# Two hundred DMA issues move from SyncE's queue to ScalarE's, and the attention tiles of the single blocks move to other steps

## The chip, the core and the metric

The kernel runs on one core of a Trainium2 chip. The metric is the device time of one execution in microseconds. Before the change the median of three runs is 741.4 us (740.5 to 743.21). The profile is of one further execution, which took 743.39 us; its instructions span 741.4 us.

## The reference

The kernel computes a chunked attention and, on its result, a mixer with two matrix products per axis:

```
S chunks of 64:  attn = softmax(q k^T / 8);  x = attn v          # 8 batches, 8 heads, 576 x 64
h = relu(x^T w_tok1) w_tok2;   u = x + h^T                       # token axis, 576 -> 256 -> 576
out = u + relu(u w_ch1) w_ch2                                    # channel axis, 512 -> 1536 -> 512
```

All data are float32. x has 512 channels (8 heads of 64), and the rows of a batch are its 576 tokens.

## The kernel before

**Tiles.** An attention tile is 128 rows by 512 columns, that is two chunks for all heads. There are 36 tiles, nine for each pair of batches. One tile takes: a load of q and k (512 KB) and of v (256 KB); the scores on TensorE (`ps_s`, or `ps_sv` L372); maximum, difference and sum on VectorE (L345, L348, L358); the exponential on ScalarE (L352); a transpose that is done by VectorE in 32 x 32 blocks (L395) and by a trip through DRAM, `far<-blocks` out (L400) and four transfers `pf<-far` back (L406); a ScalarE copy into `pt` (L423); the product with v (`ps_v` L442, or `ps_sv` L384); and a scaling into `x` (L463). The tile's x goes through the same kind of trip into `xt`, which the mixer reads.

**Stages.** Float32 products are made from a high and a low part (gh and gl, bh and bl). The profile has four stretches. In the first, to about 149 us, batch 0 is done and the weights are split; batch 1's four tiles are threaded through it by `STARTS`, whose rows are tiles and whose five columns are the steps of: scores and softmax; the trip to DRAM; the copy into `pt`; the product with v and the scaling; the end of the tile. Steps of this stretch count two for each of 12 features f (the first for `us[0]`, the second for `us[1]`), then one per f. In the second stretch, 149 to 335 us, two single blocks of 512 rows go through the channel products: 48 steps (`now`), an even one for `ch1` (12 matmuls, `ps_c` L682) and an odd one for `ch2` of the feature before (12 matmuls, `acc` L726). `BURSTS` lists the steps after which one attention step (a "burst") is issued: scores of tile `order[k]` and the product with v of tile `order[k-2]`, in one go. One step ahead of a burst stands `before` (the copy into `pt`), one step behind it `behind` (the four `pf<-far`). `TOKENS_AT` are the steps of the token products of batches 2, 3 and 4 (`ps_t` L581), `MIX_AT` those of the mix that opens the first pair (`ps_t` L653, VectorE u L660, and its splits L1091 to L1098). `SUMS` are the steps at which GpSimd adds halves of the channel weights into `sparts` (one buffer; L1008, L1017), ScalarE and GpSimd split them (L1023, L1024), and four transfers `w<-sparts` (`dump`, L881, two per step) take them to DRAM. The third and fourth stretch, to the end, are three pairs of blocks: each group of seven products (`ps_p` L1051) stands between halves of the second channel product (`acc` L1121), and each product needs its weights from the ring of eight buffers (`ring<-w`, `load_product`, L1041), which it asks for seven products ahead. `snap` (ScalarE L1140) takes a product out of one of two PSUM buffers.

**Order.** TensorE's order is the program's from step 35 of the first stretch on; in the steps before that a planner sets it. SyncE's (SP's) queue keeps the program's order throughout: one issue that waits holds all behind it. The orders of ScalarE, VectorE and GpSimd, after batch 0, are the planner's too; it works with its own estimates of costs; `issue_after(ins)` only says that something stands behind `ins` on its engine. All DMAs are issued from SP's queue. ScalarE's queue is in order as well.

Of the kernel before, what the change touches and what calls it, by code (L numbers as in the profile page):

```python
# [8 lines left out]
F32 = mybir.dt.float32  # L9
# [37 lines left out]
KH = 2 * P  # L47
RING = 8
LAG = 2
BURSTS = (2, 6, 9, 13, 17, 20, 23, 26, 30, 34, 37, 38, 40, 43)  # L50
PAIR_BURSTS = {0: (1, 9, 13, 19, 22, 30, 33, 38, 41), 1: (4, 11, 22, 28), 2: ()}
PAIR_GAPS = (1, 3)
SINGLE_GAPS = (1, 1)
TOKENS_AT = (19, 35, 44)
MIX_AT = (44, 45)
PAIR_TOKENS = ((4, 7), (4, 0), ())
PAIR_MIX = ((7, 9), (7, 9))
# [3 lines left out]
DUMPS = 2  # L61
# [16 lines left out]
END_FILL = (3, 2, 2, 3, 6, 1, 1)  # L78
STEP_FILL = (2, 4, 4, 4, 4, 4, 4, 2, 0, 2, 5, 3, 0, 8, 5, 4, 4, 5, 7, 4, 1, 1, 5, 3)

STARTS = ((9, 10, 10, 10, 14), (13, 14, 15, 16, 16), (17, 18, 18, 19, 22), (23, 23, 24, 26, 27))
SPLIT_AT = (30, 25, 32, 33, 30)
FIRST_TOKENS = (9, 10)
HAND_FROM = 11
# [2 lines left out]
JOBS = [(9, "ready")]  # L87
JOBS += [(s, "part", j, k) for j, ss in enumerate(STARTS) for k, s in enumerate(ss)]
JOBS += [(s, "split", i) for i, s in enumerate(SPLIT_AT)]
# [18 lines left out]
def attention_mixer_kernel(ctx, tc, qk_in, vo_in, v_in, w1_in, w2_in, wc1_in, wc2_in, out):  # L108
# [19 lines left out]
    nc = tc.nc  # L128
# [170 lines left out]
            xts[k] = pool.tile([P, N // BK, NDT, BK], F32, tag="xt", name="xt")  # L299
        return xts[k]  # L300

    def load_qk(i):
        qk = pool.tile([P, 2, NHP, P], F32, tag="qk" if i > 4 else "qk0", name="qk", bufs=3 if i > 4 else 5)
        nc.sync.dma_start(out=qk.rearrange("p a b c -> p (a b c)"), in_=qk_in[i])
        tiles[i] = {"qk": qk}

    def load_v(i):
        if i < NTILE:
            v = pool.tile([P, VPAD], F32, tag="v1" if i > 4 else "v0", name="v", bufs=2 if i > 4 else 5)
            v = v[:, :VW].rearrange("p (a b c) -> p a b c", a=2, c=DV)  # L310
            src = vo_in[i]
        else:
            v = pool.tile([P, 2, NHP, D], F32, tag="v", name="v", bufs=4)
            src = v_in[i - NTILE]
        nc.sync.dma_start(out=v.rearrange("p a b c -> p (a b c)"), in_=src)
        tiles[i]["v"] = v

    def attn_load(i):
        load_qk(i)
        load_v(i)  # L320

    def attn_s(i, src=None, tag="at"):
        t = tiles[i]
# [17 lines left out]
    def attn_p(i, fill=0):  # L341
        t = tiles[i]
        sv = t["s"]
        mx = per_row("mx")
        nc.vector.tensor_reduce(out=mx, in_=sv, axis=AX.X, op=ALU.max)  # L345
        convert(fill)
        pr = t["pr"] = pool.tile([P, DM], F32, tag="pr", name="pr")
        nc.vector.tensor_tensor(  # L348
            out=pr.rearrange("p (h a k) -> p a h k", a=2, k=CH), in0=sv,
            in1=mx.broadcast_to([P, 2, NHP, CH]), op=ALU.subtract,  # L350
        )
        nc.scalar.activation(out=pr, in_=pr, func=AF.Exp, scale=1.0 / float(D) ** 0.5)  # L352

    def attn_z(i):

        t = tiles[i]
        zi = t["zi"] = per_row("zs")
        nc.vector.tensor_reduce(  # L358
            out=zi, in_=t["pr"].rearrange("p (h a k) -> p a h k", a=2, k=CH), axis=AX.X, op=ALU.add
        )  # L360
        nc.scalar.activation(out=zi, in_=zi, func=AF.Copy, bias=1e-9)
        nc.vector.reciprocal(out=zi, in_=zi)

    def attn_both(i, j):

        ps = ps_at.tile([P, 2, 512], F32, tag="at", name="ps_sv")
        if i is not None:
            qk = tiles[i]["qk"]
            for hp in range(NHP):
                for a in range(2):  # L370
                    for c in range(2):
                        nc.tensor.matmul(  # L372
                            ps[c * CH:(c + 1) * CH, a, hp * CH:(hp + 1) * CH],
                            lhsT=qk[a * D:(a + 1) * D, 0, hp, c * CH:(c + 1) * CH],
                            rhs=qk[a * D:(a + 1) * D, 1, hp, c * CH:(c + 1) * CH],
                            start=True, stop=True,
                        )
            tiles[i]["s"] = ps[:, :, :NHP * CH].rearrange("p a (h k) -> p a h k", k=CH)
        if j is not None:
            t = tiles[j]  # L380
            for hp in range(NHP):
                for a in range(2):
                    for c in range(2):
                        nc.tensor.matmul(  # L384
                            ps[c * CH:(c + 1) * CH, a, (NHP + hp) * D:(NHP + hp + 1) * D],
                            lhsT=t["pt"][a * CH:(a + 1) * CH, hp, c * CH:(c + 1) * CH],
                            rhs=t["v"][a * CH:(a + 1) * CH, c, hp, :D],
                            start=True, stop=True,
                        )
            t["pv"] = ps[:, :, NHP * D:2 * NHP * D].rearrange("p a (h d) -> p a h d", d=D)  # L390
# [155 lines left out]
    def load_waiting(n):  # L546

        while waiting and n > 0:
            n -= load_x(*waiting.pop(0))
# [8 lines left out]
    def batch_tiles(b):  # L558
        base = (b // 2) * NTILE
        return [base + j for j in (range(0, 5) if b % 2 == 0 else range(5, 9))]  # L560
# [198 lines left out]

    first = batch_tiles(0)  # L760
    load_qk(first[0])
    fetch(1)
    load_v(first[0])
# [48 lines left out]
    for engine in engines:  # L812
        ins = [i for i in nc.cur_bb.bb.instructions if i.engine == engine][-1]
# [4 lines left out]
    order = [t for b in range(2, B) for t in sorted(batch_tiles(b), key=lambda t: t % NTILE != 4)]  # L818
# [55 lines left out]
    wide = ctx.enter_context(tc.tile_pool(name="wide", bufs=1, space=bass.MemoryType.DRAM))  # L874
    stored, tokens, dumps = {}, {}, []

    def dump(n):

        for key, src in dumps[:n]:
            stored[key] = wide.tile([P, 2, KH], F32, tag="w{}_{}".format(*key), name="w")  # L880
            nc.sync.dma_start(out=stored[key], in_=src if src.dtype == F32 else src.bitcast(F32))  # L881
        del dumps[:n]

# [47 lines left out]
    def attention(k):  # L931

        i = order[k] if k < len(order) else None
        j = order[k - LAG] if k >= LAG else None
        attn_both(i, j)
        if k + 2 < len(order):
            attn_load(order[k + 2])
        load_waiting(1)
        if i is not None:
            attn_p(i)  # L940
            tiles[i]["far"] = far_out(tiles[i]["pr"])
            attn_z(i)
        ready = len(waiting)
        if j is not None:
            attn_o(j)
            attn_end(j)
        load_waiting(min(2, ready))
# [88 lines left out]
    products = [(p, n) for _ in range(PAIRS) for p in range(NFC // 2) for n in range(7)]  # L1036

    def load_product(upto):
        for i in range(len(ring), min(upto, len(products))):
            w = pool.tile([P, 2, KH], F32, tag="ring", name="ring", bufs=RING)  # L1040
            nc.sync.dma_start(out=w, in_=stored[products[i]])  # L1041
            ring.append(w)

    def product(i, u, width):
# [205 lines left out]

    single_events = plan_bursts(BURSTS, len(FIRST_QK), *SINGLE_GAPS)
    events, taken = {}, len(FIRST_QK) + len(BURSTS)
    for n in range(PAIRS):
        events[n] = plan_bursts(PAIR_BURSTS[n], taken, *PAIR_GAPS)
        taken += len(PAIR_BURSTS[n])
    for k in range(SINGLE):
        at, width = BLOCKS[k]
        accs, pend = [], None
        for f in range(NFC):
            for half in range(2):  # L1260
                if half == 0:
                    g = ch1(u, f, width=width)
                elif pend is not None:
                    ch2(*pend)
                if half == 1:
                    pend = (S + at, width, u, f, g, accs)
                now = 2 * (NFC * k + f) + half
                if now in TOKENS_AT:
                    b = 2 + TOKENS_AT.index(now)
                    batch_split(b)  # L1270
                    if b != 3:
                        load_waiting(99)
                    rs[b] = [tok1(b, m) for m in range(NT1)]
                if now in MIX_AT:
                    mix_pair(SINGLE, rs, MIX_AT.index(now))
                if now == OPEN_AT[0]:
                    open_x(1)
                if now == OPEN_AT[1]:
                    open_x(SINGLE, SINGLE + 1)
                if RING_AT <= now < RING_AT + RING - 1:  # L1280
                    load_product(now - RING_AT + 1)
                if now in TOKENS_TO:
                    store_token()
                for kind, at_k in single_events.get(now, ()):
                    calls[kind](at_k)
                dump(DUMPS)
                for p, (add, cut, put) in enumerate(SUMS):
                    for when, step in ((add, add_sums), (cut, split_sums)):
                        if now == when:
                            with in_turn():  # L1290
                                step(p)
                    if now == put:
                        dump_sums(p)
        dump(len(dumps) if k else 1)
        if k == 0:
            u = turn(1, rs)
        ch2(*pend)
# [57 lines left out]
```

## Time and profile before

| | |
|---|---|
| median of three runs | 741.4 us (740.5 to 743.21) |
| the profiled execution | 743.39 us |
| its span | 741.4 us |
| TensorE busy (PE) | 717.3 us, 97% |
| VectorE, ScalarE, GpSimd busy | 437.1, 275.4, 189.6 us |
| DMA | 139.94 MB, mean 189 GB/s |
| chain that ended last | PE 74%, DMA 8%, DVE 6%, ACT 5%, SPq 4% |

PE is a matmul, DVE is VectorE, ACT is ScalarE, POOL is GpSimd, SP is SyncE; a name with q is the engine's queue (an issue or a wait), which isn't counted as busy. The granted clock (PEclk) is the share of TensorE's full speed. "Idle before" is an engine's time without work ahead of an instruction, and the arrow names what ended it.

### The profile page before, as it was taken

How to read it: one execution, taken by the hardware profiler on the slowest of the kernel's cores; microseconds unless marked ns; L12 is line 12 of the kernel's file. 1: busy time of each engine (PE TensorE's matmuls, PEld its weight loads, DVE VectorE, ACT ScalarE, POOL GpSimd, SP SyncE). 2: the span in 40 equal slices, each digit the busy share in tenths (PEclk: the TensorE clock that was granted, in tenths of full speed). 3: DMA queues.
4: the chain of work that ended last, by engine and by line, in shares of the span. 5: the costliest groups of instructions: out<-in, count | busy, mean ns of one | idle time of the engine just before them, and what ended most of it. 6: DMA issues, size and time to landing. Idle time of an engine off the chain costs nothing.

```text
span 741.4 us, 14629 instructions
## 1 busy us (share of the span) xinstructions
PE 717.3 (97%) x5730; PEld 629.7 (85%) x5730; DVE 437.1 (59%) x735; ACT 275.4 (37%) x505; POOL 189.6 (26%) x161
## 2 busy tenths in 40 slices
PE   6899998999999999989999999999999999999997
PEld 4488898988889877878888888988888899999997
DVE  4799966555546546577666763686343539433361
ACT  5899953333332333332333333332211324112120
POOL 0000012162346543103111163061112602311220
PEclk8999999999999999999999999999999999999999
DMA  9956346669855676745888995045655430644111
GB/s 344 407 218 222 118 157 198 218 202 290 289 178 185 202 229 224 237 127 197 268 261 272 284 312 139 12 140 161 192 177 182 138 93 21 235 135 126 53 54 53
DMA packets 93268, 139.94 MB, mean 189 GB/s; under 512 B 10832, under 2 KB 44880, under 8 KB 93200
## 3 DMA queue, kind: packets, MB, share of 16 engines
q1 hardware_dynamic: 93200, 139.02, 57.0%
q8 instruction: 45, 0.74, 0.4%
q14 instruction: 23, 0.19, 0.1%
HBM read 98.34 MB, written 39.71 MB: 186 GB/s over the span
## 4 chain that ended last, share of the span: by engine, by line
PE 74%; DMA 8%; DVE 6%; ACT 5%; SPq 4%; issue 2%; POOL 0%; DVEq 0%; ACTq 0%; POOLq 0%
PE acc L1121 24%; PE ps_p L1051 21%; PE acc L726 8%; PE ps_c L682 7%; PE ps_t L653 5%; PE ps_t L581 4%; SPq L406 2%; DMA far<-blocks 2%; PE ps_sv L372 2%; PE ps_sv L384 1%; DMA raw_t<-in_w 1%; DVE wtop L225 1%; ACT low L206 1%; PE sum L590 1%; ACT wtop L205 1%
## 5 line engine op out<-in xcount | busy, mean ns | idle before, releaser
L1121 PE MATMUL acc<-gh,kept_c 128*128 128x512 f32 (+1 forms) x576 | 169.5, 376 | 0.0
L1051 PE MATMUL ps_p<-bh,ring 128*128 128x512 f32 (+1 forms) x504 | 148.5, 376 | 0.1
L1121 PEld LDWEIGHTS acc<-gh,kept_c 128*128 128x128 f32 x576 | 108.2, 189 | 12.8
L1121 PE MATMUL acc<-gl,kept_c 128*128 128x512 f32 (+1 forms) x288 | 107.9, 375 | 0.0
L1051 PEld LDWEIGHTS ps_p<-bh,ring 128*128 128x128 f32 x504 | 94.6, 189 | 11.8 <-DVE sum L1146 0.5
L1051 PE MATMUL ps_p<-bl,ring 128*128 128x512 f32 (+1 forms) x252 | 94.4, 375 | 0.0
L726 PE MATMUL acc<-gh,kept_c 128*128 128x288 f32 (+1 forms) x384 | 91.1, 341 | 1.7 <-ACT gh L695 1.5
L484 POOL TENSOR_TENSOR xl<-x,xh 128x512 fp32r<-128x512 f32 x28 | 37.7, 1358 | 160.4 <-ACT xh L483 137.2
L726 PEld LDWEIGHTS acc<-gh,kept_c 128*128 128x128 f32 x384 | 63.7, 192 | 8.2 <-ACT gh L695 2.8
L1148 POOL TENSOR_TENSOR sum<-snap,sum 128x512 f32<-128x512 f32 (+1 forms) x18 | 23.1, 1282 | 167.4 <-ACT snap L1140 144.7
L1121 PEld LDWEIGHTS acc<-gl,kept_c 128*128 128x128 f32 x288 | 54.4, 189 | 6.5
L682 PE MATMUL ps_c<-uh,kept_c 128*128 128x512 f32 x192 | 57.8, 383 | 1.3 <-DVE rl L600 1.3
L726 PE MATMUL acc<-gl,kept_c 128*128 128x288 f32 (+1 forms) x192 | 57.1, 336 | 0.0
L1051 PEld LDWEIGHTS ps_p<-bl,ring 128*128 128x128 f32 x252 | 47.6, 189 | 5.7
L1153 ACT ACTIVATE gh<-c 128x512 fp32r<-128x512 f32 (+1 forms) x36 | 22.4, 622 | 77.3 <-DVE c L1146 73.4
L352 ACT ACTIVATE pr<-pr 128x512 f32<-128x512 f32 x36 | 22.6, 628 | 76.6 <-DVE pr L348 76.6
L1140 ACT COPY snap<-ps_p 128x512 f32<-128x512 f32 (+1 forms) x36 | 20.8, 577 | 75.5 <-PE ps_p L1051 71.9
L1154 DVE SCALAR_TENSOR_TENSOR gl<-g,gh 128x512 fp32r<-128x512 f32 (+1 forms) x36 | 32.9, 936 | 24.4 <-ACT gh L1153 24.4
L696 DVE SCALAR_TENSOR_TENSOR gl<-ps_c,gh 128x512 fp32r<-128x512 f32 (+1 forms) x36 | 21.8, 605 | 40.1 <-ACT gh L695 40.0
L682 PE MATMUL ps_c<-both,kept_c 128*128 128x288 f32 x288 | 41.2, 291 | 1.0 <-DVE gl L696 1.0
L682 PEld LDWEIGHTS ps_c<-uh,kept_c 128*128 128x128 f32 x192 | 35.7, 189 | 6.8 <-DVE rl L600 1.7
L682 PEld LDWEIGHTS ps_c<-both,kept_c 128*128 128x128 f32 x288 | 37.2, 189 | 2.2 <-DVE gl L696 1.4
(134 smaller groups left out, 1257.8 us busy)
## 6 DMA issues: line engine op xcount, KB each, us to landing
ring<-w SPq DMA_DIRECT2D x126, 256.0 KB, 4.0
qk<-in_qk SPq DMA_DIRECT2D x36, 512.0 KB, 4.8
far<-blocks SPq DMA_DIRECT2D x63, 256.0 KB, 2.9
raw_c<-in_wc SPq DMA_DIRECT2D x24, 512.0 KB, 9.3
pf<-far SPq DMA_DIRECT2D x124, 64.0 KB, 2.4
v<-in_v SPq DMA_DIRECT2D x27, 256.0 KB, 4.6
xt<-far SPq DMA_DIRECT2D x96, 64.0 KB, 2.0
w<-sparts SPq DMA_DIRECT2D x24, 256.0 KB, 2.7
```

Source lines behind the costliest of these rows:

```text
L352: nc.scalar.activation(out=pr, in_=pr, func=AF.Exp, scale=1.0 / float(D) ** 0.5)
L484: nc.gpsimd.tensor_tensor(out=xl, in0=t["own"], in1=xh.bitcast(F32), op=ALU.subtract)
L581: nc.tensor.matmul(ps, lhsT=lhsT, rhs=in_turn_of_two(rhs), start=(n == 0 and q == 0), stop=(n == len(mt) - 1 and q == len(terms) - 1),)
L653: nc.tensor.matmul(ps[:, at:at + n], lhsT=lhsT[:, cols], rhs=rhs.rearrange("p (c a b) -> p c b a", a=2, b=RUN), start=(q == 0), stop=(q == ...
L682: nc.tensor.matmul(ps[:, :width], lhsT=weights["c1", f][:, wi, k // 2, k % 2 * P:(k % 2 + 1) * P], rhs=in_turn_of_two(u[ui][k]), start=(k ...
L696: nc.vector.scalar_tensor_tensor(out=halved(gl), in0=ps, scalar=0.0, in1=halved(gh.bitcast(F32)), op0=ALU.max, op1=ALU.subtract)
L726: nc.tensor.matmul(accs[e], lhsT=weights["c2", f][:, wi, e * P:(e + 1) * P], rhs=in_turn_of_two(g[gi]), start=(f == 0 and q == 0), stop=(f ...
L1051: nc.tensor.matmul(ps, lhsT=w[:, wi, j * P:(j + 1) * P].bitcast(F32R), rhs=in_turn_of_two(u[ui][j]), start=j == 0 and q == 0, stop=j == 1 ...
L1121: nc.tensor.matmul(accs[e], lhsT=weights["c2", f][:, wi, e * P:(e + 1) * P], rhs=in_turn_of_two(g[gi]), start=start and q == 0, stop=stop ...
L1148: engine.tensor_tensor(out=c, in0=a, in1=b, op=ALU.add)
L1153: nc.scalar.activation(out=gh, in_=c, func=AF.Relu)
L1154: nc.vector.scalar_tensor_tensor(out=gl, in0=c, scalar=0.0, in1=gh.bitcast(F32), op0=ALU.max, op1=ALU.subtract)
```

## The change

The loads of q, k and v that an attention step asks for (two tiles ahead), the loads of the ring, and the dumps of the sums are issued from ScalarE's queue, each behind the ScalarE instruction that the program wrote last before it. The other issues stay on SP. From the ninth on, the single blocks' bursts have other steps; batch 3's token product is at step 36 (before: 35); of batch 1's four tiles the last one's steps are 22, 22, 24, 27, 28 (before: 23, 23, 24, 26, 27).

```diff
-BURSTS = (2, 6, 9, 13, 17, 20, 23, 26, 30, 34, 37, 38, 40, 43)
+BURSTS = (2, 6, 9, 13, 17, 20, 23, 26, 29, 32, 34, 37, 39, 42)
-TOKENS_AT = (19, 35, 44)
+TOKENS_AT = (19, 36, 44)
-STARTS = ((9, 10, 10, 10, 14), (13, 14, 15, 16, 16), (17, 18, 18, 19, 22), (23, 23, 24, 26, 27))
+STARTS = ((9, 10, 10, 10, 14), (13, 14, 15, 16, 16), (17, 18, 18, 19, 22), (22, 22, 24, 27, 28))
+    def on_scalar():
+        ins = [i for i in nc.cur_bb.bb.instructions if i.engine == nc.scalar.engine][-1]
+        return tc.issue_after(ins)
-    def load_qk(i):
+    def load_qk(i, queue=nc.sync):
...
-        nc.sync.dma_start(out=qk.rearrange("p a b c -> p (a b c)"), in_=qk_in[i])
+        queue.dma_start(out=qk.rearrange("p a b c -> p (a b c)"), in_=qk_in[i])
...
-    def attn_load(i):
-        load_qk(i)
-        load_v(i)
+    def attn_load(i, queue=nc.sync):
+        load_qk(i, queue)
+        load_v(i, queue)
...
-    def dump(n):
+    def dump(n, late=False):
...
+            if late:
+                with on_scalar():
+                    nc.scalar.dma_start(out=stored[key], in_=src if src.dtype == F32 else src.bitcast(F32))
+                continue
...
-            attn_load(order[k + 2])
+            with on_scalar():
+                attn_load(order[k + 2], nc.scalar)
...
-            nc.sync.dma_start(out=w, in_=stored[products[i]])
+            with on_scalar():
+                nc.scalar.dma_start(out=w, in_=stored[products[i]])
...
-                dump(DUMPS)
+                dump(DUMPS, True)
...
-        dump(len(dumps) if k else 1)
+        dump(len(dumps) if k else 1, True)
```

## Rows read from the trace of the kernel before

**Rows 1.** The page: busy time, share of the span, instructions, by engine.

```profile
PE 717.3 (97%) x5730; PEld 629.7 (85%) x5730; DVE 437.1 (59%) x735; ACT 275.4 (37%) x505; POOL 189.6 (26%) x161
```

**Rows 2.** TensorE's waits: us in total, times, longest us.

```profile
PE ps_t L653 <- DVE u L660: 3.1, 1, 3.1
PE ps_v L442 <- ACT pt L423: 2.3, 2, 2.0
PE ps_c L682 <- DVE rl L600: 1.3, 1, 1.3
PE ps_sv L384 <- ACT pt L423: 1.0, 1, 1.0
```

**Rows 3.** Three windows: us, busy of each engine, granted clock, DMA.

```profile
124.00:128.00 4.00, 4.00 (x47) 3.88 (x48) 3.29 (x7) 1.46 (x4) 1.07 (x1) 0.57 1.00 365
...
281.00:285.00 4.00, 3.03 (x58) 2.35 (x61) 3.81 (x8) 2.54 (x5) 1.27 (x1) 1.00 0.43 161
...
325.00:330.00 5.00, 4.80 (x25) 4.81 (x26) 3.83 (x7) 1.28 (x3) 1.60 (x1) 0.66 0.04 15
```

**Rows 4.** The chain of waits, 85 to 137 us: start, us, what.

```profile
107.86 2.94 PE ps_c L682 x24
...
111.17 0.67 PE ps_s L329 x32
...
115.02 4.71 DMA far<-blocks
...
121.11 1.96 DMA pf<-far
```

**Rows 5.** ScalarE's instructions in order, 262 to 285 us: start, us, what.

```profile
271.39 1.04 ACT L1023 CAST sparts<-sparts 128x1024 fp32r<-128x1024 f32 x1 [4.22 <-POOL sparts L1017]
...
272.45 1.07 ACT L599 ACTIVATE rh<-ps_t 128x512 fp32r<-128x512 f32 x2
...
284.06 0.62 ACT L423 COPY pt<-pf 128x512 f32<-128x512 f32 x1
```

**Rows 6.** GpSimd's instructions in order, 255 to 276 us.

```profile
268.44 1.42 POOL L1017 TENSOR_TENSOR sparts<-wsum 128x256 f32<-128x256 f32 x2 [8.19 <-DMA w<-sparts]
```

**Rows 7.** SP's issues in order, 239 to 268 us.

```profile
259.82 4.32 SPq L406 DMA_DIRECT2D xt<-far  x8
264.18 2.11 SPq L881 DMA_DIRECT2D w<-sparts  x2
```

**Rows 8.** SP's issues in order, 296 to 322 us.

```profile
301.65 0.40 SPq L1041 DMA_DIRECT2D ring<-w  x1
305.55 1.74 SPq L406 DMA_DIRECT2D pf<-far  x4
...
307.81 0.90 SPq L881 DMA_DIRECT2D w<-sparts  x2
...
309.28 0.57 SPq L304 DMA_DIRECT2D qk<-in_qk  x1
...
310.39 2.40 SPq L406 DMA_DIRECT2D xt<-far  x4
```

**Rows 9.** VectorE's instructions in order, 311 to 326 us.

```profile
318.31 0.69 DVE L660 TENSOR_TENSOR u<-ps_t,xt 128x512 f32<-128x512 f32 x1 [4.04 <-DMA xt<-far]
...
324.46 0.68 DVE L660 TENSOR_TENSOR u<-ps_t,xt 128x512 f32<-128x512 f32 x1
```

**Rows 10.** SP's waits: us in total, times, longest us.

```profile
SPq L1041 <- PE ps_p L1051: 57.7, 26, 8.0
```

**Rows 11.** DMA issues of the page: count, KB each, median us to landing.

```profile
ring<-w SPq DMA_DIRECT2D x126, 256.0 KB, 4.0
```

**Rows 12.** The chain of waits over the whole span.

```profile
245.78 2.59 PE acc L726 x12
...
346.91 1.29 PE acc L1121 x6
348.21 1.29 PE ps_p L1051 x6
```

**Rows 13.** Group of a line: count, busy us, mean ns, idle before.

```profile
L1140 ACT COPY snap<-ps_p 128x512 f32<-128x512 f32 (+1 forms) x36 | 20.8, 577 | 75.5 <-PE ps_p L1051 71.9 <-DMA ring<-w 3.6
```

More of the change, by code (lines that the diff above doesn't have):

```diff
@@ L300, in block_x, with load_v @@
         return xts[k]
-    def load_qk(i):
+    def on_scalar():
+        ins = [i for i in nc.cur_bb.bb.instructions if i.engine == nc.scalar.engine][-1]
+        return tc.issue_after(ins)
+    def load_qk(i, queue=nc.sync):
         qk = pool.tile([P, 2, NHP, P], F32, tag="qk" if i > 4 else "qk0", name="qk", bufs=3 if i > 4 else 5)
-        nc.sync.dma_start(out=qk.rearrange("p a b c -> p (a b c)"), in_=qk_in[i])
+        queue.dma_start(out=qk.rearrange("p a b c -> p (a b c)"), in_=qk_in[i])
         tiles[i] = {"qk": qk}
-    def load_v(i):
+    def load_v(i, queue=nc.sync):
         if i < NTILE:
@@ L314, in load_v @@
             src = v_in[i - NTILE]
-        nc.sync.dma_start(out=v.rearrange("p a b c -> p (a b c)"), in_=src)
+        queue.dma_start(out=v.rearrange("p a b c -> p (a b c)"), in_=src)
         tiles[i]["v"] = v
-    def attn_load(i):
-        load_qk(i)
-        load_v(i)
+    def attn_load(i, queue=nc.sync):
+        load_qk(i, queue)
+        load_v(i, queue)
     def attn_s(i, src=None, tag="at"):
```

## The prediction

> **What bounds the kernel now.** I read the page first: TensorE is busy 97% of the span, ScalarE 37% [rows 1]. So the kernel is as long as TensorE's work plus its stops, and no edit here takes a matmul away; only stops can go. TensorE's waits come next [rows 2]. Behind batch 0 there are four of any size: 3.1 us for VectorE's u in the mix, 2.0 us for pt in `ps_v` (the longest of the two in its row), 1.3 us for rl, 1.0 us for pt in `ps_sv`. [...] A stretch costs (1 - 0.57) x 4 = 1.7 us and (1 - 0.66) x 5 = 1.7 us. So what can be had is 2.0 + 1.7 (A), 1.3 (B), 1.0 (C) and 3.1 + 1.7 (D): 10.8 us, 1.5% of 741.4.
>
> What ended each stop stands in the chain and in the engines' own rows.
>
> A, at 122 us: the last tile of batch 1. Its scores start at 111.17, its trip out is issued at 115.02 and takes 4.71, the way back is issued by 121.11 [rows 4]; then comes ScalarE's copy, and `ps_v` waits 2.0.
>
> B, at 272 us: ScalarE reaches rh of batch 3's token product at 272.45, because L1023 ahead of it waited 4.22 us for GpSimd [rows 5]. GpSimd had waited 8.19 us for a dump to free `sparts` [rows 6]. SP issued that dump at 264.18, behind eight xt issues that took 4.32 [rows 7]. It is a backlog of SP, three engines away from TensorE.
>
> C, at 284 us: the burst of step 38, one step behind that of step 37; its pt is copied at 284.06 [rows 5].
>
> D, at 322 us: u at 318.31 stood 4.04 us for xt, and VectorE, with its row of splits, gets to the u that frees TensorE's buffer at 324.46, 6.15 us later [rows 9]. That xt was issued at 310.39, behind ring, dump, qk and v issues and behind four pf that had to wait to 305.55 [rows 8].
>
> **The change part by part.**
>
> *Last tile of batch 1 (A).* Scores one step earlier means ahead of twelve `ps_c` matmuls: half of 2.94, 1.5 us [rows 4]. The product with v one step later means one more group of twelve behind it, another 1.5. Together 3.0, more than the 2.0 missing. But the planner sets TensorE's order here and need not follow both. With one of the two in effect, 0.5 us of the stop is left and it is shorter than C's 1.0, around which the clock held: gain 1.5 + 1.7 = 3.2. With both: 3.7. With neither: 0. I take 3.4. Scores also need the PSUM buffer of the tile before; that binds the first of the two moves, not the second. The tile's end comes a step later (28); the token product that reads it is at steps 33 and 34, so nothing there is close.
>
> *Batch 3's token product (B).* At step 36 it stands behind a `ch1` instead of a `ch2`, so that a `ch2` of 2.59 us [rows 12] separates its second sum from the next `ch1`, which needs the buffer. 2.59 exceeds 1.3. Independently of that the dump leaves SP's backlog. Either is enough: I take the whole 1.3 (bounds 0 and 1.3).
>
> *Bursts (C, D).* The burst of step 38 goes to 39, and its tile's scores stay at a distance of five steps (34) instead of four; no two bursts are nearer than two steps, where 37 and 38 stood at one. C goes: 1.0 (bounds 0 and 1.0). The last burst goes from 43 to 42, and with it the issue of the xt that D waits for: 2.59 us earlier against the mix. In front of that xt SP loses three ring issues of 0.40, two dumps of 0.90 together, qk 0.57 and a v like it [rows 8]: some 3.1 us. 2.59 + 3.1 = 5.7, more than the 4.04 that it was late. So D goes: 3.1 + 1.7 = 4.8 (bounds 0 and 4.8). What is late next is TensorE's own sum for the following u, so nothing new appears there. Work is only moved: every burst, product and transfer is still done once, also in the steps where bursts now stand closer (32 and 34).
>
> *The issues in ScalarE's queue.* 25 tiles x 2 loads, 126 ring loads [rows 11] and 24 dumps are 200 issues. The trace has no issue of ScalarE's; the nearest are SP's, 0.40 to 0.57 each, 0.43 where four stand in a row [rows 8]. That is 86 us of ScalarE over 600. Lower end: 0, as ScalarE is idle for 466 us [rows 1]. Upper end: 86, if each stood on the path. A gain below 0 is excluded, since behind 335 us no wait of TensorE is left that an earlier load could shorten.
>
> Each issue also waits, and ScalarE's later work queues behind it. A v load waits for the burst that it is traced with (its buffer's reader is that burst's product); behind it stand the exponential of the same burst, which needs the burst anyway, and the gh of the next `ch1`. That gh has until `ch2` two pieces later, 2 x 2.59 less a ScalarE and a VectorE instruction of some 0.6 to 0.7 [rows 5, 9]: 3.9 us. A burst's two loads and two dumps come to 1.7. A ring load waits for the product that frees its buffer; on SP that came to 57.7 us over 26 waits [rows 10]. Behind it on ScalarE stands `snap`, but of the next product: the wait ends before snap's own input is there. snap has 0.58 us of work [rows 13] and must be done before the second product behind it, that is within two pieces of 1.29 [rows 12]: 2.0 us to spare, four issues long. So most of the 86 us is covered by ScalarE's idle time; if the cover fails somewhere, a stop like C or B appears. I take one such stop, 1.3 us, nearer to 0 than to 86 because the idle time is five times the issues.
>
> *Sum.* 3.4 + 1.3 + 1.0 + 4.8 = 10.5, less 1.3 = 9.2. On the profiled execution: span 741.4 to 732.2, and with the 2.0 around the span 743.39 to 734.2. The median of the three runs lies 2.0 below that execution, at 741.4, so the forecast for the median is 732.2.
>
> **The rivals.**
>
> *The planner leaves A where it is.* For: `ps_v` is not at its step now. Its step, 26, ends three groups of the second loop, and the chain shows it behind pt alone; TensorE's place is where the planner believed pt to be there. A later step may then change nothing, and earlier scores may be held by the PSUM buffer. Against: the way out took 4.71 [rows 4] and would be issued earlier if the scores are. Time: 741.4 - (10.5 - 3.4) + 1.3 = 735.6.
>
> *Many short holds on ScalarE.* Issues are not always 0.43: two dumps took 2.11 [rows 7]. If each of the 25 steps that load a tile adds 0.3 us to TensorE, as a gh or a copy comes late, that is 7.5: 741.4 - 10.5 + 7.5 = 738.4. For: loads, dumps and ring loads meet in steps 41 to 47, beside the mix. Against: 3.9 us of slack there. [...]
>
> [...]
>
> *The change doesn't do what it says in D*: xt stays late because its trip out is late, not its issue. The burst's step alone then gives 2.59 of the 3.1: 0.5 is left, the clock holds, D gives 4.3 instead of 4.8. 732.7, within the likeliest case.
>
> **How the numbers follow.** The likeliest case is that all four stops go or nearly so, at 732.2, with 730.6 (10.8 and nothing added) to 734.5 around it: 0.51, the last rival in it. A stays: 0.19. Many short holds: 0.18. Slower: 0.12. Half a per cent, 3.7 us, is what a measurement of this kernel can tell from no change. Faster by more than that (under 737.7): 0.51, 0.17 of A's 0.19, 0.05 of the holds' 0.18: 0.73. Within: 0.02 + 0.12 + 0.02 = 0.16. Slower: 0.01 + 0.10 = 0.11. The range ends below at 730.6 less 1.8 for the spread of single runs (741.4 against 743.21), 728.8, and above at 741.5, which takes in A's and the holds' cases and leaves out the slower one.
>
> **What would show it.** Right: TensorE's waits have no row over 1 us behind 100 us; the two windows behind `ps_v` and the mix show clock 1.00; L1017 no longer waits 8 us for w<-sparts; VectorE's u doesn't wait for xt; the pairs take as long as before. A is wrong if `ps_v` still waits for pt; the slack is wrong if ps_p or acc wait for snap or gh, or if ScalarE's issues stand over 2 us. The prediction is wrong if the time is over 737.7.

## The result: slower, and the profile after

| | before | after |
|---|---|---|
| median of 4 executions (range), us | 741.49 (740.5 to 743.21) | 749.51 (748.27 to 753.23) |
| profiled execution, us (span) | 743.39 (741.4) | 749.17 (747.4) |

The ratio of the times is 1.0119, with a 95% interval of 1.0087 to 1.015. The forecast was 732.2, so it had the wrong sign. (A ratio here can differ by a thousandth or two from the quotient of the medians.) One execution of before, timed beside the experiments, was in a slow state, 928.75 us at a mean granted clock of 0.75, and is in none of the ratios below.

The views follow in the order of the prediction. First the page's busy line by engine (busy us, share, instructions), which answers to [rows 1]:

```profile
PE 717.3 (96%) x5730; PEld 630.0 (84%) x5730; DVE 438.2 (59%) x735; ACT 275.1 (37%) x505; POOL 188.3 (25%) x161
```

The instruction counts are those of before. So only stops, and the clock behind them, can have changed. TensorE's waits (us in total, times, longest), against [rows 2]:

```profile
PE ps_sv L389 <- ACT pt L428: 11.3, 2, 10.3
...
PE ps_v L447 <- ACT pt L428: 3.0, 2, 2.7
...
PE acc L731 <- DVE gl L701: 0.7, 1, 0.7
```

The waits for u in the mix (D, 3.1) and for rl (B, 1.3) are no longer among these. The wait of `ps_v` for pt (A) is still there, 2.7 instead of 2.0. And one wait is new: 10.3 us of a burst's product with v for pt, where before no wait of `ps_sv` was longer than 1.0. The windows around it (length, busy us and instructions by engine, granted clock, DMA share, GB/s), and the one behind A:

```profile
123.00:127.00 4.00, 3.38 (x43) 3.27 (x44) 2.60 (x6) 2.17 (x5) 0.24 (x1) 0.57 1.03 368
...
266.00:277.00 11.00, 0.68 (x36) 0.54 (x40) 3.71 (x7) 3.40 (x7) 0.00 (x0) 0.68 0.74 214
277.00:281.00 4.00, 4.00 (x41) 3.35 (x42) 2.94 (x6) 1.21 (x2) 0.14 (x1) 0.59 0.26 88
```

TensorE works 0.68 us of the eleven from 266 to 277. Behind the stop the granted clock is 0.59 for 4 us (0.50 from 278 to 280), which by an estimate from that window costs (1 - 0.59) x 4 = 1.6 us more.

To see where the time went, I cut each profile at the same matmuls: the last `ps_s` of the first tiles, the first 512-wide `ps_c` (first single block), the first `ps_c` of the second single block, the first `ps_p` (pairs). Lengths in us:

| kernel | start | to block 0 | block 0 | block 1 | pairs |
|---|---|---|---|---|---|
| before | 111.6 | 37.8 | 84.6 | 103.7 | 403.7 |
| after | 110.5 | 38.8 | 86.7 | 108.0 | 403.4 |
| steps_only | 110.1 | 36.2 | 84.6 | 111.2 | 403.7 |
| bursts_only | 110.6 | 37.1 | 84.6 | 109.6 | 403.4 |
| late_rest | 111.0 | 37.9 | 87.0 | 101.7 | 403.4 |
| late_rest_loads_sp | 110.6 | 36.3 | 84.6 | 101.9 | 403.8 |
| late_rest_open33 | 110.8 | 36.9 | 85.1 | 98.6 | 403.4 |
| ring_dumps | 109.9 | 36.5 | 84.6 | 98.4 | 404.8 |

(The lower six are experiments, below.)

After against before: -1.1 + 1.0 + 2.1 + 4.3 - 0.3 = 6.0, the difference of the spans. (The start varies from 109.9 to 113.6 over all profiles, so nothing is read from it.) Block 1 holds B, C and D, 7.1 us that should have gone, to 96.6. With 10.3 + 1.6 for the new stop that is 108.5, and 108.0 was measured. So block 1 is as long as B, C and D gone and one new stop in their place make it. That each of the three went for the reason that I gave doesn't follow from the sum: the new stop stands ahead of all three, and everything behind it had ten more microseconds.

What made the stop? TensorE's timeline (start, length, engine, line; in brackets the idle time before and what ended it) shows its place, the burst of step 34:

```profile
265.90 0.70 PE L377 MATMUL ps_sv<-qk 64*64 64x64 f32 x32
276.92 1.13 PE L389 MATMUL ps_sv<-v,pt 64*64 64x64 f32 x32 [10.32 <-ACT pt L428]
```

ScalarE's timeline of the same stretch, from 265 to the copy (one small instruction left out):

```profile
265.20 0.63 ACT L357 ACTIVATE pr<-pr 128x512 f32<-128x512 f32 x1 [4.89 <-DMA qk<-in_qk]
265.74 1.23 ACT L509 CAST stack<-x 64x512 fp32r<-64x512 f32 x2
...
267.29 0.58 ACT L700 ACTIVATE gh<-ps_c 128x512 fp32r<-128x512 f32 x1
269.75 0.34 ACTq L309 DMA_DIRECT2D qk<-in_qk  x1
275.09 0.61 ACT L515 CAST xr<-xc 64x512 fp32r<-64x512 f32 x1 [7.22 <-DMA xc<-x]
275.55 0.33 ACTq L320 DMA_DIRECT2D v<-in_v  x1
275.73 0.62 ACT L515 CAST xr<-xc 64x512 fp32r<-64x512 f32 x1
276.25 0.61 ACT L428 COPY pt<-pf 128x512 f32<-128x512 f32 x1
```

The copy to pt is one instruction of 0.61 us, but ahead of it in ScalarE's order stands xr, the rest of the stack of the tile whose burst ran at step 32, and xr stood 7.22 us for the transfer of xc. SP's queue says why xc was so late:

```profile
258.48 6.93 SPq L411 DMA_DIRECT2D xt<-far  x8
265.50 2.18 SPq L411 DMA_DIRECT2D pf<-far  x4
267.73 1.85 SPq L411 DMA_DIRECT2D xt<-far  x4
269.68 0.38 SPq L405 DMA_DIRECT2D far<-blocks  x1
270.15 1.12 SPq L506 DMA_DIRECT2D xc<-x  x2
```

Eight xt issues took 6.93 us. Behind them stand the pf for this burst (issued from 265.50, the last landed at 269.73) and xc (issued from 270.15, its first half landed at 275.07). So the stop has two layers: until 269.75 pt could not start because pf was late, 3 to 4 us of the stop; the other 6.5 are pt behind xr. VectorE stood for xr too:

```profile
275.79 1.40 DVE L516 TENSOR_TENSOR stack<-xc,xr 64x512 fp32r<-64x512 f32 x2 [7.20 <-ACT xr L515]
```

Had the same wait been in the kernel before? Yes, and the prediction did not look at it. ScalarE's timeline of before:

```profile
275.27 1.26 ACT L510 CAST xr<-xc 64x512 fp32r<-64x512 f32 x2 [1.75 <-DMA xc<-x]
```

There xc landed 12.7 us behind its burst (after: 15.7). But that burst was at step 34 and the next at 37, with the token product between them 16.6 us later, so the pt behind xr was still in time. With the bursts at 32 and 34, the work behind the one (xr) and ahead of the other (pt) falls on the same step 33, in the order in which the planner lists it: xr first.

Block 0 lost 2.1 us elsewhere. ScalarE's timeline there, and the issue of SP that belongs to it (two views of after):

```profile
188.72 0.37 ACTq L309 DMA_DIRECT2D qk<-in_qk  x1
193.74 0.34 ACTq L320 DMA_DIRECT2D v<-in_v  x1
194.13 0.63 ACT L357 ACTIVATE pr<-pr 128x512 f32<-128x512 f32 x1 [8.37 <-DMA pf<-far]
```

```profile
188.16 1.96 SPq L411 DMA_DIRECT2D pf<-far  x4
```

ScalarE's issue of v left 5 us after that of qk, 0.02 us after the second of these four pf had landed (issued at 188.83, landed at 193.72). The exponential behind it ran at 194.13 (before: 189.83, with block 0 starting within 0.1 us of the same time), and gh, pt and gl after it: 0.7 us of stop at `acc` and 1.0 at `ps_sv`.

### The profile page after: what moved, and what is told of

Same layout as the page of the kernel before. It is cut to its first block, busy times and chain, and to the rows that moved or that the text cites. A ratio compares the mean times of both kernels' runs of the same rounds, so it can differ in the third digit from the quotient of the medians.

```text
span 747.4 us, 14542 instructions
## 1 busy us (share of the span) xinstructions
PE 717.3 (96%) x5730; PEld 630.0 (84%) x5730; DVE 438.2 (59%) x735; ACT 275.1 (37%) x505; POOL 188.3 (25%) x161
## 4 chain that ended last, share of the span: by engine, by line
PE 73%; DMA 10%; ACT 5%; DVE 5%; issue 3%; SPq 2%; POOL 1%; ACTq 0%; DVEq 0%; POOLq 0%
PE acc L1132 25%; PE ps_p L1062 22%; PE ps_t L658 6%; PE ps_t L586 6%; PE ps_c L687 6%; PE acc L731 5%; DMA pf<-far 2%; SPq L411 2%; DMA xt<-far 2%; PE ps_sv L389 1%; PE ps_sv L377 1%; DMA raw_t<-in_w 1%; DMA w<-kept_c 1%; ACT low L206 1%; DMA xc<-x 1%
## 5 line engine op out<-in xcount | busy, mean ns | idle before, releaser
L1132 PEld LDWEIGHTS acc<-gh,kept_c 128*128 128x128 f32 x576 | 108.4, 189 | 12.7
L1132 PE MATMUL acc<-gl,kept_c 128*128 128x512 f32 (+1 forms) x288 | 108.0, 375 | 0.0
L1165 DVE SCALAR_TENSOR_TENSOR gl<-g,gh 128x512 fp32r<-128x512 f32 (+1 forms) x36 | 33.4, 952 | 23.1 <-ACT gh L1164 16.6
L1165 DVE SCALAR_TENSOR_TENSOR gl<-c,gh 128x512 fp32r<-128x512 f32 (+1 forms) x36 | 25.1, 699 | 24.2 <-ACT gh L1164 24.1
```

Of the source, the lines that this page charges most:

```text
L1132: nc.tensor.matmul(accs[e], lhsT=weights["c2", f][:, wi, e * P:(e + 1) * P], rhs=in_turn_of_two(g[gi]), start=start and q == 0, stop=stop ...
L1165: nc.vector.scalar_tensor_tensor(out=gl, in0=c, scalar=0.0, in1=gh.bitcast(F32), op0=ALU.max, op1=ALU.subtract)
```

## The experiments

Each was timed beside before, four kernels at a time. Medians of before there: 739.35 (first four), 738.23 (next four), 738.92 (next four), 737.74 (last four). No difference reaches 2%; slower, level and faster go by whether the 95% interval, in brackets, lies over 1, takes it in, or lies under it.

### queue_only

After with the old steps.

```diff
+BURSTS = (2, 6, 9, 13, 17, 20, 23, 26, 30, 34, 37, 38, 40, 43)
+TOKENS_AT = (19, 35, 44)
+STARTS: last row (23, 23, 24, 26, 27)
```

> The issues in ScalarE's queue, with all steps of before. Theory 1 (the new steps put behind and before on one step, so that the copy into pt stands in ScalarE's queue behind the stack's xr, which waits for its xc transfer): the stop of 10.3 us does not appear; what ScalarE's issues do by themselves shows at 196 to 201 us, some 2 us; 738 to 743 us. Theory 2 (ScalarE's issues wait for landings and hold pt): a stop of 5 us or more in a burst's product with v, 746 to 751 us.

745.24 us, ratio 1.0076 [1.0046, 1.0106]. The queue alone makes the kernel slower, and neither expectation had the time right. The stop of 10.3 us isn't there. Of the old stops B is 0.7, C 0.9, D gone; new ones lie in block 1. TensorE's waits, and ScalarE's copy behind the longest of the first row:

```profile
PE ps_sv L389 <- ACT pt L428: 3.8, 3, 2.3
PE ps_t L586 <- ACT xh L488: 1.9, 1, 1.9
```

```profile
293.94 0.62 ACT L428 COPY pt<-pf 128x512 f32<-128x512 f32 x1 [3.91 <-DMA pf<-far]
```

### steps_only

Before with the three new step tuples; every issue stays on SP.

```diff
+BURSTS = (2, 6, 9, 13, 17, 20, 23, 26, 29, 32, 34, 37, 39, 42)
+TOKENS_AT = (19, 36, 44)
+STARTS: last row (22, 22, 24, 27, 28)
```

> The new steps with every issue on SP's queue, as before the change. Theory 1: the long stop at the burst of step 34 is there as well, 8 to 12 us, and the time is 746 to 752 us. Theory 2: no stop over 4 us behind 130 us, stops B, C and D gone: 731 to 736 us.

747.43 us, 1.0106 [1.0072, 1.014], as theory 1 had it. The long stop is there with no issue on ScalarE at all:

```profile
PE ps_sv L384 <- ACT pt L423: 12.5, 2, 11.9
```

So the stop belongs to the steps, not to the queue. A is 0.4 here, block 0 has its old 84.6.

### pt_first

After, with the work ahead of a burst listed before the work behind one.

```diff
+        for jobs in at.values():
+            jobs.sort(key=lambda job: job[0] != "before")
         return at
```

> The changed kernel, with before ahead of behind where both fall on one step, so that the copy into pt is traced ahead of the stack's xr (steps 33 and 38, and one step of the first pair). Theory 1: the stop falls from 10.5 us to what the late pf transfer alone makes (it landed 3.4 us behind the burst's scores): 742 to 744 us. Theory 2: the stop stays within 2 us of 10.5, 747 to 750 us.

746.66 us, 1.0081 [1.0053, 1.011], slower than the 742 to 744 of theory 1. TensorE's waits and ScalarE's timeline:

```profile
PE ps_sv L389 <- ACT pt L428: 4.7, 1, 4.7
PE ps_t L586 <- DVE gl L701: 2.1, 1, 2.1
```

```profile
268.17 0.62 ACT L428 COPY pt<-pf 128x512 f32<-128x512 f32 x1 [3.20 <-DMA pf<-far]
...
274.07 0.62 ACT L515 CAST xr<-xc 64x512 fp32r<-64x512 f32 x1 [4.68 <-DMA xc<-x]
```

pt now goes first and waits for pf alone: the stop falls from 10.3 to 4.7, which is the layer of pf. But xr still holds ScalarE, and VectorE with it, now ahead of the gh and gl that the token product at step 36 needs: 2.1 us of a new stop. Block 1 is 107.6, the gain only 0.4.

### burst_35

After with the burst of 34 at 35, three steps behind the one before.

```diff
+BURSTS = (2, 6, 9, 13, 17, 20, 23, 26, 29, 32, 35, 37, 39, 42)
```

> The changed kernel with the burst of step 34 at step 35, so that before and behind no longer share a step there, and one more step lies between its tile's scores and the product with v. Theory 1: no stop over 2 us behind 130 us: 733 to 739 us. Theory 2: the stop only moves, 745 to 750 us.

746.66 us, 1.0107 [1.008, 1.0134]: theory 2, the stop only moves.

```profile
PE ps_t L586 <- DVE gl L701: 5.4, 1, 5.4
PE ps_sv L389 <- ACT pt L428: 1.3, 1, 1.3
```

The burst is nearly free, and the token product takes its place: its second sum waits 5.4 us for a gl. The way back from that gl: its gh (277.76) stands in ScalarE's order behind the exponential (276.64), which waited for VectorE, which had waited 7.60 us for xr (272.97), and xr 4.14 for xc. Moving pt away from xr is not enough, since everything behind xr is late.

### late_rest

After, with the rest of that tile's stack (xr and VectorE's part) two bursts later, behind that of step 37 instead of that of 32.

```diff
+RESTS = {11: (), 13: (11, 13)}
...
-                stack_end(j)
+                for r in RESTS.get(k, (k,)):
+                    stack_end(order[r - LAG])
```

> The changed kernel, with the stack's rest (xr, L515, and its VectorE half) of batch 4's first tile traced behind the burst of step 37 instead of that of step 32, so that nothing that waits for the xc transfer stands ahead of a burst's pt. Theory 1 (xr, which waits for xc, blocks ScalarE's and VectorE's queues ahead of pt): the stop at the burst of step 34 falls from 10.5 us to the 3 to 4 us that its late pf transfer makes; ratio to before 1.000 to 1.005. Theory 2 (the late pf transfer alone holds it): the stop stays over 8 us, ratio over 1.009.

742.83 us, 1.0047 [1.0027, 1.0068]. TensorE's wait, and ScalarE's timeline:

```profile
PE ps_sv L390 <- ACT pt L429: 4.6, 2, 3.7
```

```profile
269.50 0.62 ACT L429 COPY pt<-pf 128x512 f32<-128x512 f32 x1 [2.14 <-DMA pf<-far]
```

Block 1 falls from 108.0 to 101.7. So xr and its half on VectorE, at that place, were worth 6.3 us, and pt_first had shown that it is xr ahead of pt that holds the burst: that is the cause of the larger layer. The rest of the stop, 3.7, is pf, as in pt_first.

### steps_late_rest

The same edit on steps_only, that is with all issues on SP.

```diff
+RESTS = {11: (), 13: (11, 13)}
...
```

> The same edit with all issues on SP's queue and the new steps. Theory 1: the stop of 12 us falls to 3 to 5 us, ratio 0.998 to 1.004. Theory 2: it stays over 9 us, ratio over 1.008.

739.41 us, 1.0009 [0.9986, 1.0031]. The stop falls from 11.9 to 3.0, block 1 from 111.2 to 101.7. Against late_rest, timed beside it, 742.83 - 739.41 = 3.4 us is the price of ScalarE's issues at equal steps. (With the old steps, queue_only against before, it is 5.9.)

### tok_starts

Before with the new step of the token product and the last tile of batch 1, with the old bursts.

```diff
+TOKENS_AT = (19, 36, 44)
+STARTS: last row (22, 22, 24, 27, 28)
```

> The kernel before with two of the four parts alone: batch 3's token product at step 36 and the new steps of batch 1's last tile; bursts and queue as before. If these two are harmless: stop B is gone, stop A stays because TensorE's order there is the planner's, 1 to 2 us faster than before, ratio 0.997 to 1.000. If one of them carries part of the loss: ratio over 1.004.

743.2 us, 1.0051 [1.0022, 1.008]. TensorE's waits, then ScalarE's timeline and VectorE's:

```profile
PE ps_t L581 <- DVE gl L696: 4.4, 1, 4.4
```

```profile
272.74 0.61 ACT L510 CAST xr<-xc 64x512 fp32r<-64x512 f32 x1 [2.12 <-DMA xc<-x]
273.38 0.60 ACT L695 ACTIVATE gh<-ps_c 128x512 fp32r<-128x512 f32 x1
```

```profile
274.73 0.69 DVE L696 SCALAR_TENSOR_TENSOR gl<-ps_c,gh 128x512 fp32r<-128x512 f32 x1
```

With the old bursts the new step 36 loses. The second sum needs the PSUM buffer that gl has to read first, and gl comes after gh, gh after xr, xr after xc. B's 1.3 us were exchanged for 4.4. A, with the new last row, is 0.5. D's wait is 0.3, though the burst that it hangs on is still at 43; that xt has 4.4 us more time behind this stop would explain it.

### late_rest_open33

late_rest, with the first pair's x opened at step 33 instead of 26, so that its xt issues leave SP's backlog of 258 to 268 us.

```diff
-OPEN_AT = (1, 26)
+OPEN_AT = (1, 33)
```

> late_rest with blocks 2 and 3 opened at step 33 instead of 26, so that fewer xt issues stand on SP ahead of the pf of the bursts at 29, 32 and 34. If SP's backlog of xt makes that pf late: no stop over 1.5 us at these bursts, 3 us faster than late_rest, ratio 0.994 to 1.000. If not: the stops and the time of late_rest. The xt that are missing may come late for the mix instead (u waits for xt).

739.34 us, 1.0003 [0.9983, 1.0024]. The pf for the burst of step 34 and the xc of the stack in SP's queue, first in late_rest, then here:

```profile
264.81 2.92 SPq L412 DMA_DIRECT2D pf<-far  x4
...
270.20 1.11 SPq L507 DMA_DIRECT2D xc<-x  x2
```

```profile
254.02 2.23 SPq L412 DMA_DIRECT2D pf<-far  x4
...
260.87 1.67 SPq L507 DMA_DIRECT2D xc<-x  x2
```

The burst's scores start at 265.81 in late_rest and at 262.66 here. So pf left 1.0 us ahead of them there and 8.6 here, the stop at this burst is gone, and block 1 is 98.6. So the layer of pf was SP's backlog of xt. A wait of 1.7 us for pt is new, at the burst of step 42. It is the first version with ScalarE's issues that is level with before.

### steps_late_open33

The same with every issue on SP.

```diff
 (steps_late_rest)
+OPEN_AT = (1, 33)
```

> New steps, the stack's rest at the burst of step 37, blocks 2 and 3 opened at 33, every issue on SP's queue. Theory 1 (the loss is the stack's rest and SP's xt backlog ahead of the bursts at 32 and 34; ScalarE's queue adds its own loss and saves nothing): no stop over 2 us behind 130 us, the first single block 84.6 us as before, 734 to 737 us, ratio 0.992 to 0.998, and no slower than the same kernel with ScalarE's issues (ratio 1.0003). Theory 2 (ScalarE's issues are what lets the xt come in time): a stop of 2 us or more comes back at the bursts of 32 to 37 or in the mix, ratio 1.000 or more.

738.37 us, 0.9985 [0.9966, 1.0004]; the longest such stop is 1.9, at the burst of step 42. Level with before, at the edge of a gain, and slower than the 734 to 737 that I had expected.

### ring_dumps

late_rest_open33 with the loads of q, k and v back on SP; ring loads and dumps stay on ScalarE.

```diff
-            with on_scalar():
-                attn_load(order[k + 2], nc.scalar)
+            attn_load(order[k + 2])
```

> The changed kernel with the stack's rest late and blocks opened at 33, with only the ring loads and the dumps in ScalarE's queue; the attention loads go back to SP. If the loads' waits for earlier landings are what holds ScalarE (the exponential behind a v issue): the first single block falls from 85.1 to 84.6 us and the time to that of the same kernel on SP, within 0.3%. If the dumps or the ring hold it: stops by gh or pt stay at 190 to 202 us.

737.26 us, 0.9973 [0.9954, 0.9993]: the best, and the only one whose interval lies below 1.

```profile
PE ps_t L659 <- DVE u L666: 1.0, 1, 1.0
...
PE ps_sv L390 <- ACT pt L429: 0.4, 1, 0.4
```

Block 0 is at its old 84.6, block 1 at 98.4. In this profile the 126 ring loads and the dumps in ScalarE's queue cost TensorE no more than the 1.1 us by which the pairs are longer, and part of even that may be the execution.

### old_steps_late_open33, old_steps_open33

Before with the later xt, with and without the later rest of the stack.

```diff
+RESTS = {11: (), 13: (11, 13)}     (first of the two only)
+OPEN_AT = (1, 33)
```

> The kernel before (old steps, all on SP), with the stack's rest at the burst of step 38 and blocks 2 and 3 opened at 33. If the two edits alone carry the gain: stops B, C and D gone, ratio 0.990 to 0.996. If the even steps are needed too: C or D stays, ratio 0.997 to 1.001.

> The kernel before with blocks 2 and 3 opened at 33 alone. If SP's backlog of xt was behind stops B and D: both gone, 0.993 to 0.998. If not: 0.998 to 1.002, with a stop in the mix where xt come later still.

742.27 us, 1.0053 [1.003, 1.0076], and 742.55 us, 1.0056 [1.0034, 1.0077]. Both are slower than before and than I had expected, with waits of 3.4 and 3.5 us for pt at the burst of step 40; C is there as before, and without the later rest u still waits 2.7 in the mix (0.6 with it). The two mends that make the new steps as good as before make the old ones worse: eight xt issues now stand ahead of the pf for the burst of 40. The even spacing is of use only once rest and xt are out of its way.

### loads_on_sp, late_rest_loads_sp

After, and late_rest, with only the loads of q, k and v back on SP.

```diff
-            with on_scalar():
-                attn_load(order[k + 2], nc.scalar)
+            attn_load(order[k + 2])
```

> The changed kernel with the attention loads back on SP; ring loads and dumps stay in ScalarE's queue. Theory (the loads' waits for SP's landings hold ScalarE): no stop at 190 to 202 us, first single block 84.6 us, but the long stop at the burst of step 34 stays (8 to 12 us): ratio 1.006 to 1.011. Rival (dumps and ring hold it as much): the stops at 196 and 200 stay.

> late_rest with the attention loads back on SP. Theory: 84.6 us in the first single block, a stop of 3 to 4 us left at the burst of step 34 (late pf), ratio 0.999 to 1.003, where late_rest had 1.0047. Rival: ratio 1.004 or more.

746.33 us, 1.0105 [1.0081, 1.013], and 739.48 us, 1.002 [0.9997, 1.0042]. Block 0 is 84.6 in both instead of 86.7 and 87.0, so the loss there belongs to these 50 issues. The long stop stays in the first, as it must:

```profile
PE ps_sv L389 <- ACT pt L428: 10.9, 2, 9.9
```

### bursts_only

Before with the new bursts alone.

```diff
+BURSTS = (2, 6, 9, 13, 17, 20, 23, 26, 29, 32, 34, 37, 39, 42)
```

> The kernel before with the new bursts alone. Theory (burst 32 with the stack's tile, and the next burst two steps behind it, make the long stop): a stop of 8 to 13 us at the burst of step 34, ratio 1.007 to 1.013. Rival (the token product at 36 is needed for it): no stop over 5 us there, ratio under 1.005.

747.99 us, 1.0135 [1.0106, 1.0164].

```profile
PE ps_sv L384 <- ACT pt L423: 10.2, 2, 9.9
```

One tuple of numbers alone makes a loss as large as that of the whole change (1.0119). A is 2.1 with it, as before.

### ring_dumps_open30

ring_dumps with xt from step 30.

```diff
-OPEN_AT = (1, 33)
+OPEN_AT = (1, 30)
```

> ring_dumps with blocks 2 and 3 opened at 30 instead of 33. If the two waits for u (1.1 and 1.2 us) came from xt that were asked for late, and the backlog ahead of the bursts at 32 and 34 stays small: both waits gone, 2 us faster, ratio 0.993 to 0.997. If the backlog returns: a stop of 2 to 4 us at the burst of step 34, ratio 0.999 to 1.003.

742.24 us, 1.0045 [1.0025, 1.0064]. A stop of 3.4 us for pt is back, but at another burst than I had expected, that of step 42 (its product with v starts at 299.20). Eight xt issues from 289.34 stand ahead of its pf (294.08). Once more a burst lacks the pf that stands behind eight xt issues of SP.

## Why the prediction was wrong

Forecast -9.2 us, profiled +6.0: 15.2 apart. By stage that is block 1 (forecast -7.1, measured +4.3) 11.4, A (-3.4 against +1.0) 4.4, the added issues (1.3 against 2.1) 0.8, less 1.4 in the start and the pairs.

*Bursts (C, D): the step that failed.* "Work is only moved ... also in the steps where bursts now stand closer (32 and 34)" looked at TensorE's distance of two steps and priced the rest at nothing. I had not listed what a burst leaves on ScalarE behind it. A burst's tail (xr, waiting for a transfer) and the next one's head (pt) now share a step in an in-order queue: pt, whose pf had landed at 269.73, ran at 276.25, behind both xr. What it cost was a stop of 10.3 us and, by the estimate above, 1.6 us of lower clock. bursts_only and steps_only show that the steps alone make the stop, late_rest that xr is 6.3 us of it, late_rest_open33 that SP's backlog is the rest. C's own gain came: the bursts of 37 and 39 do not wait, in ring_dumps neither, where no long stop stands ahead of them. D is gone in after, and the granted clock there is 1.00:

```profile
324.00:330.00 6.00, 6.00 (x42) 5.68 (x40) 5.17 (x9) 2.09 (x5) 0.00 (x0) 1.00 0.01 3
```

That it went by the mechanism given is not shown. The wait is also gone in queue_only (burst at 43, issues off SP) and in steps_late_open33 (burst at 42, issues on SP, no stop over 1.9), so either part can do it; and in after the stop ahead of it gave xt ten more microseconds as well. My sum for it was off too: of the three ring issues that I took off, the one at 301.65 stands ahead of the four pf that waited to 305.55 [rows 8] and held nothing back, so that some 2.7 are left of the 3.1.

*Token product (B).* "Either is enough" was wrong. tok_starts lost 4.4 us at step 36, where the gh and gl of the `ch1` ahead have to be done by then. I had followed the buffer on TensorE's side (2.59 against 1.3) and not the two engines that free it. The dump's part was right: GpSimd's wait at L1027 ended sooner, 2.26 us and on another transfer, against the 8.19 of [rows 6]:

```profile
262.81 1.41 POOL L1027 TENSOR_TENSOR sparts<-wsum 128x256 f32<-128x256 f32 x2 [2.26 <-DMA xt<-far]
```

*Last tile of batch 1 (A).* The rival's reason was right: scores and `ps_v` stand at the same place in TensorE's order as before; the scores start 4.5 us behind the `ps_v` of the tile before in both. Yet the stop can go, by way of the transfers: with the new row and the q, k and v loads on SP it is 0.4 to 1.1 in eight profiles, with the old row 1.8 to 2.1 in five, before among them. In all five a store `w<-kept_c` is SP's issue right ahead of the trip out (in before at 114.46, the trip at 115.02); with the new row it stands behind. With the new row and those loads on ScalarE the stop was 0.2 in one profile and 1.3 to 2.7 in four. ScalarE's queue cannot be the reason: its first issue comes only when the copy that ends the stop is under way (after):

```profile
122.95 0.62 ACT L428 COPY pt<-pf 128x512 f32<-128x512 f32 x1 [6.90 <-DMA pf<-far]
123.13 0.39 ACTq L309 DMA_DIRECT2D qk<-in_qk  x1
```

To 118 us after and steps_only have the same instructions in the same order on every engine. Why the trip out takes 4.70 us in the one and 3.33 in the other is open.

*The issues in ScalarE's queue.* 1.3 was forecast, block 0 lost 2.1, and the price at equal steps by medians is 3.4 with the rest late, 5.9 at the old steps, and none between steps_only and after, each some 8 us over its before, where the long stop covers it. The 25 issues of qk on ScalarE last 0.33 to 0.47 us, 0.34 in the median, less than the 0.43 that I took; what costs is the wait inside the queue, which I had weighed only for ring loads and for the readers of a buffer. The v load waited for another queue's transfer instead, 5 us, which the prediction had named as a sign that its slack is wrong (over 2 us). The case called slower (0.12) rests on a term that no run shows. The result lies on its side, but by the bursts: in after the pairs took 403.4 us against 403.7, and the 71 of ScalarE's 200 issues that overlap one of SP's last 0.37 us in the median, the 129 others 0.33.

*What could be had.* The 10.8 us were read from one execution of 743.39 us, whose mean granted clock was 0.988. The 113 executions of before that the ratios of the experiments rest on ran from 735.1 to 744.2, with medians near 738.5. In 41 of them the mean granted clock was 0.998 or more (median time 737.7), in 21 it was 0.988 or less (740.3). By an estimate from [rows 3], two stretches that lose 1.7 us each bring the mean over 741 us to 0.995, so those 41 cannot have had both: part of my 10.8 is not in every execution of before. The sum puts 1.7 us of lower clock, from the windows of [rows 3] at 0.57 and 0.66, down to the stops A and D; no run shows that such a stretch has to follow a stop of 2 us or more. In old_steps_late_open33 pt stops TensorE for 2.1 us ahead of 123.1 and for 3.4 ahead of 291.6, and the granted clock stays at 1.00:

```profile
122.00:127.00 5.00, 3.87 (x61) 3.66 (x64) 3.06 (x7) 2.24 (x5) 0.84 (x1) 1.00 0.87 295
...
292.00:296.00 4.00, 4.00 (x41) 3.50 (x33) 3.45 (x6) 1.40 (x4) 1.73 (x3) 1.00 1.06 352
```

ring_dumps has lost nearly all of A to D in its profile (735.97) and gains 1.7 us by medians, not 7. How much of the four waits themselves the median execution of before has is open: only the one execution was profiled.

## What to carry to other kernels

Before moving a piece of work closer to another, list for every in-order queue what the first leaves behind and the second sends ahead, and what each instruction there waits for; a wait for xc that cost nothing where the next burst came 16.6 us later cost 6.5 us where it came two steps later. A stop can have more than one layer, and the first mend shows the next: here xr (6.3 us, late_rest), then pf (3.7 there), then gl (2.1 in pt_first). An issue put in a working engine's queue can cost, beside its own third of a microsecond (0.34 us), what it waits for: in block 0 of after v left 5.0 us behind qk. And a stop that vanishes behind a longer one has not been shown to be mended.

## What the runs showed of the hardware

ScalarE's issue of v in block 0 stood until a transfer issued by SP had landed, 0.02 us before, though it shares no data with it. In before SP's 677 issues signal eight semaphores in turn, 84 or 85 times each; I read the wait as that of an issue for the eighth one before it, whichever queue that came from. In the trace of after the issue of v waits for one semaphore alone, the one that this pf raises when it lands and that v raises next. It fits pt_first too: there the same pf was issued at 188.27, 0.44 us ahead of ScalarE's qk (in after at 188.83, 0.11 behind it), landed at 190.46 after 2.2 us instead of 4.9, and v left at 190.48, again 0.02 behind it and in time for no stop to follow. Tenths of a microsecond between two queues decided over 2. That the loads cause block 0's loss is shown (loads_on_sp); the semaphores as its mechanism were read from the program and not tried by themselves.

The trip of pf, median from issue to landing, is longer in the profiles named here that have these loads on ScalarE (the page's DMA issues of after, then of steps_only, KB each and us):

```profile
pf<-far SPq DMA_DIRECT2D x124, 64.0 KB, 3.8
```

```profile
pf<-far SPq DMA_DIRECT2D x124, 64.0 KB, 2.5
```

It is 3.8 and 3.9 in queue_only and late_rest, 2.4 and 2.8 in loads_on_sp and late_rest_loads_sp, while the median of the 96 xt of the same size stays at 2.0 to 2.1 throughout. That median hides a difference, as nearly half of these xt lie behind 335 us. From 110 to 335 us the trips divide by whether a load of q, k or v was under way when they were issued. In before that holds for 28 of 44 xt, which took 4.4 us in the median, against 2.0 for the other 16; and for none of the 68 pf (2.2), because SP issues pf ahead of the loads. In after it holds for 26 of the 68 pf, which took 4.5, against 2.4 for the other 42. In loads_on_sp it holds for no pf again (2.1). So in these kernels the longer trip is the one that starts under a load. xt bore this already in before; with the loads in a second queue pf bears it too.
